# Attention scores as pairs of 64-row products, a weight check moved to late in the program, and a layer in halves

## The chip, the cores and the metric

One core of a Trainium2 chip runs the whole program. The metric is the time of one execution in device microseconds. Three timed runs of the kernel before gave 632.48, 632.51 and 632.81 us; their median, 632.51 us, is the time before. The engines that matter are PE (TensorE, the matrix engine; its loads of weights are listed as PEld), DVE (VectorE), ACT (ScalarE), POOL (GpSimd) and SP, whose queue issues all DMAs.

## What is computed

Attention over a short window with a few "sink" keys, then two feed-forward layers, on 2 x 768 tokens:

```python
batch, n_heads, seq, head_dim = (2, 8, 768, 64);  n_sink, window = (4, 128)
scores = scale * np.matmul(q, k.transpose(0, 1, 3, 2))
keep = is_sink | in_window                 # the last 128 keys and the first 4
a = softmax(np.where(keep, scores, -1e9))
x = np.matmul(a, v)                        # to (1536 tokens, 512)
h = x @ w_in;  x = (h * np.tanh(log1p(exp(h)))) @ w_out      # layer 0: 512 -> 2048 -> 512
h = x @ w2_in; out = (h * clip(h + 3, 0, 6) / 6) @ w2_out    # layer 1
```

q, k and v are float32. The four weight matrices come as float64.

## The kernel before

**Units and blocks.** A unit is 128 query tokens of one batch, with all 8 heads; there are 12, units 0 to 5 of the first batch and 6 to 11 of the second. Its window lies in its own 128 keys, those of the unit before, and the sinks. The first unit of a batch has one block of keys, the second has two, all later ones have two and 16 columns of sinks. Four units make a token block of 512 tokens, the width of one product in the two layers (`BLOCKS`, line 985).

**Early attention (`First`, lines 237 to 338).** Units 0 to 7 run first, in float32: `prep` transposes q and k on PE (line 251), `scores` multiplies (line 275, contraction over the 64 numbers of a head, so 64 of PE's 128 rows; odd heads sit in rows 64 to 127), takes the masked minimum on DVE (line 276) and the exponential on ACT (line 280); `turn` transposes the weights of the softmax (line 291), `values` multiplies by v (line 317), `normalise` and `outputs` divide and transpose into `xt` (lines 326, 332). Four heads make a group; each head's scores go to a PSUM bank of the pool `ps_h` (three banks), the output `o` to the one bank of `ps_s`.

**Layers (`up`, `down`, `moe_steps`).** float32 values are held as pairs of float16, so that a product becomes three (hi x hi, hi x lo, lo x hi). A step takes two of the 16 tiles of the hidden width: `up` makes 24 products into two `ps_h` banks (lines 646 to 648), ACT and DVE make the activation (lines 650 to 670), and `down` makes 24 products into the four accumulators (line 705), one step late (`LAG = 1`). `STAGES` (line 978) sets the order: layer 0 on block 0 and 1 in parts, as weights and attention come in, then block 2, then layer 1 on blocks 0, 1 and 2, each over all 16 tiles. Where a stage does not reach tile 16, `finish` copies its sums out (line 717) and a later stage adds them (line 721).

**Weights (`gen_decode`, lines 178 to 201).** Each of 32 tiles (two loads of 512 KB) is turned from float64 bits into pairs of float16 by five DVE and two ACT operations. The first DVE operation (line 185) and one on ACT (line 186) only check that the exponents are in range; their sums decide at the very end whether a general path has to run. Two raw buffers (`STB = 2`) hold what is loaded, and the 16 decoded buffers hold one layer, so that layer 1's tiles wait until layer 0's last block has used the same buffer.

**Late attention (`gen_front`, `gen_back`).** Units 8 to 11 run beside layer 0, in pieces that `hook` calls four times a step. Keys and queries are split into float16 pairs and transposed by DMA. For scores, a head's keys lie as (hi | lo) over the 128 rows and its queries as (lo | hi), so that one product over 128 rows makes both cross terms (line 465) and a second over 64 rows makes hi x hi (line 466):

```python
for t1, w_ in segs:                      # own keys (128 columns), previous keys and sinks (144)
    nc.tensor.matmul(sp[:, c:c + w_], qt[:, h, :], t1[:, h, 0:w_], start=True, stop=False)
    nc.tensor.matmul(sp[:, c:c + w_], qh[r0:r0 + 64, h // 2, :], t1[r0:r0 + 64, h, 0:w_], start=False, stop=True)
```

**What sets the order.** Each engine runs its instructions in the order in which the tile framework's scheduler put them, and each waits on semaphores of others. All DMAs stand in one queue, SP's, in the scheduler's order. A buffer of a pool is handed on when its last reader is done.

Of the kernel before, what the change touches and what calls it, by code (L numbers as in the profile page):

```python
# [17 lines left out]
SQ = 11      # powers of two that place float32 values in the range of float16 pairs  # L18
SK = 11
# [10 lines left out]
def attention_moe_moe2(  # L30
# [41 lines left out]
    blocks = BLOCKS  # L72
    order = sum(blocks, [])
    first = [u for u in range(NU) if u in sum(blocks[:2], [])]
# [12 lines left out]
    # previous block and sinks in it | own block | previous block | sinks  # L87
# [6 lines left out]
    # what the fast path relies on: lows[:, i] at least 1 in some partition, bads[:, i] 0 in all  # L94
# [28 lines left out]
    def emit_masks():  # L123
# [6 lines left out]
        # kept: 0 <= q - k < window in the block itself  # L130
# [14 lines left out]
        # which of four heads a row of the sink chunk belongs to: (row % 64) // 16  # L145
# [18 lines left out]
    def load_w():  # L164
        if nload[0] >= len(wseq):
            return
        layer, f = wseq[nload[0]]
        nload[0] += 1
# [7 lines left out]
        raw_t[layer, f] = t  # L176

    def gen_decode(idx):
# [3 lines left out]
        # nonzero where the exponent doesn't lie in float32's range below 2  # L182
        y = dec_p.tile([128, 1024], I16, tag="y", name="y")
        top = t.rearrange("p f t -> p (f t)").bitcast(I16).rearrange("p (f t) -> p f t", t=4)[:, :, 3]
        nc.vector.tensor_scalar(out=y, in0=top, scalar1=0x7800, scalar2=0x3800, op0=ALU.bitwise_and, op1=ALU.bitwise_xor)  # L185
        nc.scalar.activation(out=y, in_=y, func=AF.Copy, accum_out=wchk[:, idx:idx + 1])  # L186
# [50 lines left out]
    class First:  # L237
# [25 lines left out]
        def scores(self, g):  # L263
# [5 lines left out]
            for hh in range(4):  # L269
                h = 4 * g + hh  # L270
                rows = slice(64 * (h % 2), 64 * (h % 2) + 64)
                sp = ps_h.tile([128, n], F32, tag="h", name="s")
# [3 lines left out]
                nc.vector.tensor_tensor_reduce(  # L276
                    out=d[:, hh, 0:n], in0=sp, in1=self.mask, scale=SCALE, scalar=BIG,
                    op0=ALU.add, op1=ALU.min, accum_out=self.mins[:, h:h + 1],
                )
                nc.scalar.activation(  # L280
                    out=d[:, hh, 0:n], in_=d[:, hh, 0:n], func=AF.Exp, scale=-1.0,
                    bias=self.mins[:, h:h + 1], accum_out=self.sums[:, h:h + 1],
                )
# [20 lines left out]
        def values(self, g):  # L304
            if g == 0:
                self.o = ps_s.tile([128, H, D], F32, tag="so", name="o")
# [95 lines left out]
    def gen_keys(u):  # L402
        # heads in pairs: keys (hi lo | lo hi); values as pairs of float16
        b, i = divmod(u, NSB)
        kn, vn = (qkv_n.pop((u, nm)) for nm in "kv")
        k16 = late["at1"].tile([128, HP, 4, D], F16, tag="k16", name="k16")
        kp = kn.rearrange("p (a b) d -> p a b d", b=2)
        khi, klo = k16[:, :, 0::3, :], k16[:, :, 1:3, :]
        nc.scalar.activation(out=khi, in_=kp, func=AF.Copy, scale=2.0 ** SK)
        for h in range(2):  # L410
            nc.vector.scalar_tensor_tensor(out=klo[:, :, h], in0=kp[:, :, h], scalar=2.0 ** SK, in1=khi[:, :, h], op0=ALU.mult, op1=ALU.subtract)
        kt[u] = late["kv"].tile([128, H, 144], F16, tag="kt1", name="kt1")
        nc.sync.dma_start_transpose(out=kt[u][:, :, 0:128], in_=k16.rearrange("p a t d -> p (a t d)"))
# [11 lines left out]
    def gen_front(u):  # L425
# [9 lines left out]
        # queries (lo hi | hi lo)  # L435
        q16 = at1_p.tile([128, HP, 4, D], F16, tag="q16", name="q16")
# [586 lines left out]
```

## Time and profile before

| | |
|---|---|
| timed runs, median | 632.51 us (632.48 to 632.81) |
| profiled execution, span from first to last instruction | 636.4 us |
| PE busy | 617.9 us, 97% of the span |
| DVE busy | 373.3 us, 59% |
| ACT busy | 363.3 us, 57% |
| SP's DMA queue | 55.23 MB, 33.1% of 16 engines |
| late score products, lines 465 and 466 | 128 |
| weight check, lines 185 and 186 | 32 on each of DVE and ACT |

The profile shows one execution; its span is 3.9 us longer than the median of the timed runs, and the page gives no other time for it. A product's recorded duration includes the way through the array, which overlaps the next product: 512 columns are listed at about 380 ns and follow each other every 0.216 us. What a product costs is therefore read from starts, not from durations.

### The profile page before, as it was taken

To read this page: it belongs to the slowest core of one execution; us is meant where nothing else is said; L and a number is where in the kernel's file an instruction comes from. 1 tells how busy PE (TensorE), PEld (TensorE's weight loads), DVE (VectorE), ACT (ScalarE), POOL (GpSimd) and SP (SyncE) were. 2 spreads that over 40 slices of the span, in tenths; PEclk is the share of its full clock that TensorE was granted. 3 is DMA by queue.
4 is the path that set the end of the run, shared out by engine and by line. 5 is a ranking of instruction groups with operands and counts; after the bars stand their busy time and mean duration, and the time that the engine had idled before them with its cause. 6 is when DMAs were issued, how large, how long until landed. Compare 5 with 4: busy or idle time off the path is not lost.

```text
span 636.4 us, 8544 instructions
## 1 busy us (share of the span) xinstructions
PE 617.9 (97%) x3336; PEld 316.8 (50%) x3336; DVE 373.3 (59%) x694; ACT 363.3 (57%) x632; POOL 15.3 (2%) x28
## 2 busy tenths in 40 slices
PE   8999999989999999999999999999999999999995
PEld 4888865434454545444444444444444444444442
DVE  4687889977998753635789889852232222222221
ACT  5687798878878865665768865532141212422221
POOL 0200000600000000000000000000000000000000
PEclk8899999989999999999999999999999999999998
DMA  9747334988658603020134532300010000100001
GB/s 191 175 87 197 96 121 117 232 190 209 151 153 182 181 14 71 18 53 0 67 132 136 181 133 81 133 1 0 1 67 0 1 0 1 66 1 2 0 1 71
DMA packets 97256, 55.85 MB, mean 88 GB/s; under 512 B 75176, under 2 KB 91560, under 8 KB 97208
## 3 DMA queue, kind: packets, MB, share of 16 engines
q1 hardware_dynamic: 97208, 55.23, 33.1%
q8 instruction: 28, 0.46, 0.3%
q14 instruction: 20, 0.16, 0.1%
HBM read 43.65 MB, written 3.15 MB: 74 GB/s over the span
## 4 chain that ended last, share of the span: by engine, by line
PE 78%; DVE 8%; ACT 7%; DMA 4%; issue 2%; SPq 1%; ACTq 0%; DVEq 0%
PE acc L705 30%; PE h L646 11%; PE h L648 11%; PE h L647 11%; PE o L317 4%; PE s L275 4%; PE tp L291 2%; PE s L466 2%; DVE w L196 1%; DVE p L189 1%; DVE e L663 1%; ACT e L658 1%; ACT y L186 1%; PE tp L251 1%; PE s L465 1%
## 5 line engine op out<-in xcount | busy, mean ns | idle before, releaser
L646 PE MATMUL h<-xt,w 128*128 128x512 f16 x384 | 145.9, 380 | 2.0 <-DVE e L663 2.0
L647 PE MATMUL h<-xt,w 128*128 128x512 f16 x384 | 145.8, 380 | 0.0
L648 PE MATMUL h<-xt,w 128*128 128x512 f16 x384 | 145.6, 379 | 0.0
L705 PE MATMUL acc<-g,w 128*128 128x512 f16 x576 | 132.5, 381 | 1.0 <-DVE g L670 0.9
L705 PE MATMUL acc<-w,g 128*128 128x512 f16 x576 | 128.1, 379 | 0.0
L652 ACT ACTIVATE e<-h,bias 128x512 f32<-128x512 f32 x48 | 32.8, 685 | 136.1 <-PE h L648 136.1
L665 DVE SCALAR_TENSOR_TENSOR e<-e,h 128x512 f32<-128x512 f32 x48 | 33.0, 687 | 128.1 <-ACT e L652 128.1
L705 PEld LDWEIGHTS <-g 128*128 128x128 f16 x576 | 56.4, 98 | 67.9
L705 PEld LDWEIGHTS <-w 128*128 128x128 f16 x576 | 54.6, 98 | 65.5 <-issue 2.7
L670 DVE SCALAR_TENSOR_TENSOR g<-e,g 128x1024 f16<-128x1024 f32 x48 | 58.7, 1223 | 27.5 <-ACT g L669 27.4
L669 ACT ACTIVATE g<-e 128x1024 f16<-128x1024 f32 x48 | 50.6, 1054 | 32.6 <-DVE e L665 20.3
L647 PEld LDWEIGHTS <-w 128*128 128x128 f16 x384 | 37.6, 98 | 45.8 <-issue 2.9
L648 PEld LDWEIGHTS <-w 128*128 128x128 f16 x384 | 37.6, 98 | 44.8
L646 PEld LDWEIGHTS <-w 128*128 128x128 f16 x384 | 37.7, 98 | 43.6 <-issue 0.3
L650 ACT ACTIVATE e<-h 128x512 f32<-128x512 f32 x48 | 28.5, 593 | 32.7 <-PE h L648 32.5
L196 DVE SCALAR_TENSOR_TENSOR w<-p,w 128x1024 f16<-128x1024 f32 x32 | 39.2, 1224 | 11.7 <-ACT w L193 11.6
L186 ACT ACTIVATE y<-y 128x1024 int16<-128x1024 int16 x32 | 33.6, 1050 | 14.0 <-DVE y L185 14.0
L189 DVE SCALAR_TENSOR_TENSOR p<-raw,p 128x1024 int32<-128x1024 int32 x32 | 39.2, 1224 | 0.6
L190 DVE SCALAR_TENSOR_TENSOR p<-raw,p 128x1024 int32<-128x1024 int32 x32 | 39.1, 1222 | 0.2
L193 ACT ACTIVATE w<-p 128x1024 f16<-128x1024 f32 x32 | 33.6, 1049 | 5.7 <-DVE p L190 5.5
L663 DVE SCALAR_TENSOR_TENSOR e<-e,h 128x512 f32<-128x512 f32 x48 | 30.8, 681 | 9.8 <-ACT e L660 9.7
L280 ACT ACTIVATE d<-d,mins 128x272 f32<-128x272 f32 (+2 forms) x64 | 30.5, 480 | 3.7 <-DVE mins L276 3.6
(142 smaller groups left out, 619.3 us busy)
## 6 DMA issues: line engine op xcount, KB each, us to landing
raw<-in_moe_w_in_dram SPq DMA_DIRECT2D x32, 512.0 KB, 3.7
raw<-in_moe_w_out_dram SPq DMA_DIRECT2D x32, 512.0 KB, 4.7
out_dram<-ob SPq DMA_DIRECT2D x12, 256.0 KB, 2.1
first<-in_k_dram SPq DMA_DIRECT2D x8, 256.0 KB, 4.9
first<-in_q_dram SPq DMA_DIRECT2D x8, 256.0 KB, 5.0
first<-in_v_dram SPq DMA_DIRECT2D x8, 256.0 KB, 4.0
nk<-in_k_dram SPq DMA_DIRECT2D x5, 256.0 KB, 3.3
nv<-in_v_dram SPq DMA_DIRECT2D x5, 256.0 KB, 4.4
```

Source lines behind the costliest of these rows:

```text
L186: nc.scalar.activation(out=y, in_=y, func=AF.Copy, accum_out=wchk[:, idx:idx + 1])
L189: nc.vector.scalar_tensor_tensor(out=p, in0=lo_w, scalar=29, in1=p, op0=ALU.logical_shift_right, op1=ALU.bitwise_or)
L190: nc.vector.scalar_tensor_tensor(out=p, in0=hi_w, scalar=-0x40000000, in1=p, op0=ALU.bitwise_and, op1=ALU.bitwise_or)
L193: nc.scalar.activation(out=w[:, :, 0, :], in_=pf, func=AF.Copy, scale=2.0 ** SW)
L196: nc.vector.scalar_tensor_tensor(out=w[:, :, 1, :], in0=pf, scalar=2.0 ** SW, in1=w[:, :, 0, :], op0=ALU.mult, op1=ALU.subtract)
L646: nc.tensor.matmul(o, wh, x[:, 0, c, :], start=c == 0, stop=False)
L647: nc.tensor.matmul(o, wh, x[:, 1, c, :], start=False, stop=False)
L648: nc.tensor.matmul(o, wl, x[:, 0, c, :], start=False, stop=c == KD - 1)
L663: nc.vector.scalar_tensor_tensor(out=e[:, i], in0=e[:, i], scalar=2.5, in1=hps[i], op0=ALU.subtract, op1=ALU.mult)
L669: nc.scalar.activation(out=gh, in_=e, func=AF.Copy, scale=sc)
L670: nc.vector.scalar_tensor_tensor(out=gl, in0=e, scalar=sc, in1=gh, op0=ALU.mult, op1=ALU.subtract)
L705: nc.tensor.matmul(o, l_, r_, start=first and m == 0 and x == 0, stop=last and end and x == 2, skip_group_check=True)
```

## The change

- **Late scores**: keys and queries are laid out with the even head of a pair in rows 0 to 63 and the odd head in rows 64 to 127, hi and lo in separate columns. Each head now makes three 64-row products per block of keys (hi x hi, hi x lo, lo x hi), and the two heads' products alternate. Both heads' banks are filled before DVE takes the minima. `qh` and its transpose are gone.
- **Early scores**: two heads' products alternate in the same way.
- **PSUM**: `ps_s` is gone, `ps_h` has four banks, shared by scores, outputs `o` and the layers' `up`.
- **Units**: block 0 is units 6, 7, 0, 1; block 1 is 2 to 5; the early attention runs in that order.
- **Weight check**: layer 0's tiles are no longer checked while they are decoded. They are loaded a second time, from stage 8 on and after the last decode, and checked then. The ACT operation reads int32 words, half as many elements.
- **Layer 1 in halves**: blocks 0 and 1 take tiles 0 to 7, then tiles 8 to 15; block 2 all 16.

```diff
-    ps_h = main.enter_context(tc.tile_pool(name="ps_h", bufs=3, space=PSUM))
-    ps_s = main.enter_context(tc.tile_pool(name="ps_s", bufs=1, space=PSUM))
+    ps_h = main.enter_context(tc.tile_pool(name="ps_h", bufs=4, space=PSUM))
...
+    def exponents(idx, t):
+        y = dec_p.tile([128, 1024], I16, tag="y", name="y")
+        top = t.rearrange("p f t -> p (f t)").bitcast(I16).rearrange("p (f t) -> p f t", t=4)[:, :, 3]
+        nc.vector.tensor_scalar(out=y, in0=top, scalar1=0x7800, scalar2=0x3800, op0=ALU.bitwise_and, op1=ALU.bitwise_xor)
+        yy = y.bitcast(I32)
+        nc.scalar.activation(out=yy, in_=yy, func=AF.Copy, accum_out=wchk[:, idx:idx + 1])
+
+    def gen_check():
+        ahead = []
+        for f in range(KF):
+            ahead.append((f, fetch_w(0, f)))
+            if len(ahead) > STB - 1:
+                g, t = ahead.pop(0)
+                exponents(g, t.rearrange("p a f t -> p (a f) t"))
+            yield
...
     def gen_decode(idx):
...
+        if layer == 1:
+            exponents(idx, t)
...
-            for hh in range(4):
...
+            for h0 in (4 * g, 4 * g + 2):
+                sps = [ps_h.tile([128, n], F32, tag="h", name="s") for _ in range(2)]
                 for m, kv in enumerate(self.kvs):
                     w_ = n - 128 if m else 128
-                    nc.tensor.matmul(sp[:, m * 128:m * 128 + w_], self.qt[rows, h // 2, :], kv[0][rows, h // 2, 0:w_], start=True, stop=True)
+                    for r in range(2):
+                        rows = slice(64 * r, 64 * r + 64)
+                        nc.tensor.matmul(sps[r][:, m * 128:m * 128 + w_], self.qt[rows, h0 // 2, :], kv[0][rows, h0 // 2, 0:w_], start=True, stop=True)
...
-                sp = ps_s.tile([128, n], F32, tag="so", name="s")
...
+                sps = [ps_h.tile([128, n], F32, tag="h", name="s") for _ in range(2)]
                 c = 0
                 for t1, w_ in segs:
-                    nc.tensor.matmul(sp[:, c:c + w_], qt[:, h, :], t1[:, h, 0:w_], start=True, stop=False)
-                    nc.tensor.matmul(sp[:, c:c + w_], qh[r0:r0 + 64, h // 2, :], t1[r0:r0 + 64, h, 0:w_], start=False, stop=True)
+                    for tq, tk in ((0, 0), (0, 1), (1, 0)):
+                        for r in range(2):
+                            rows = slice(64 * r, 64 * r + 64)
+                            nc.tensor.matmul(
+                                sps[r][:, c:c + w_], qt[rows, tq * HP + h0 // 2, :], t1[rows, tk * HP + h0 // 2, 0:w_],
+                                start=tq + tk == 0, stop=tq == 1,
+                            )
...
-            ob = part_p.tile([128, DM], F32, tag="part", name="ob")
+            ob = a if span[0] > 0 else part_p.tile([128, DM], F32, tag="part", name="ob")
...
+            budget["chk"] = stage >= CHECK and not raw_t
...
-STAGES = [(0, 0, 0, 4), (0, 1, 0, 10), (0, 0, 4, 16), (0, 1, 10, 16), (0, 2, 0, 16), (1, 0, 0, 16), (1, 1, 0, 16), (1, 2, 0, 16)]
+STAGES = [(0, 0, 0, 4), (0, 1, 0, 10), (0, 0, 4, 16), (0, 1, 10, 16), (0, 2, 0, 16), (1, 0, 0, 8), (1, 1, 0, 8), (1, 0, 8, 16), (1, 1, 8, 16), (1, 2, 0, 16)]
+CHECK = 8
...
-BLOCKS = [[0, 1, 2, 3], [4, 5, 6, 7], [8, 9, 10, 11]]
+BLOCKS = [[6, 7, 0, 1], [2, 3, 4, 5], [8, 9, 10, 11]]
```

How this moves instructions is seen at three places. On PE, the scores of a late head before, between products of `up` (lines 646 and 648); `s` is the head's bank, `kt1` and `qt`, `qh` the transposed keys and queries:

```order
L648 MATMUL h_1632<-xt1_92,w_1230 128x512
L465 LDWEIGHTS qt_1519
L465 MATMUL s_1577<-kt1_1466,qt_1519 128x128
L466 LDWEIGHTS qh_1520
L466 MATMUL s_1577<-kt1_1466,qh_1520 128x128
L465 LDWEIGHTS qt_1519
L465 MATMUL s_1577<-kt1_1420,qt_1519 128x144
L466 LDWEIGHTS qh_1520
L466 MATMUL s_1577<-kt1_1420,qh_1520 128x144
```

Now, the first half of the first pair of late heads at the same kind of place:

```order
L668 MATMUL h_1500<-xt1_89,w_1111 128x512
L480 LDWEIGHTS qt_1489
L480 MATMUL s_1517<-kt1_1439,qt_1489 128x128
L480 LDWEIGHTS qt_1489
L480 MATMUL s_1518<-kt1_1439,qt_1489 128x128
L480 LDWEIGHTS qt_1489
L480 MATMUL s_1517<-kt1_1439,qt_1489 128x128
L480 LDWEIGHTS qt_1489
L480 MATMUL s_1518<-kt1_1439,qt_1489 128x128
```

Four products of one head have become twelve of two heads, which stand together with nothing between them at all 16 places and alternate between two banks.

On DVE, the middle of layer 1 before, where the last decode is over (line 665 is the activation of an `up` bank, line 670 the float16 remainder that `down` waits for):

```order
L670 SCALAR_TENSOR_TENSOR g_3938<-e,g_3938 128x1024
L196 SCALAR_TENSOR_TENSOR w<-p,w 128x2x512
L665 SCALAR_TENSOR_TENSOR e<-e,h 128x512 x2
L670 SCALAR_TENSOR_TENSOR g_4022<-e,g_4022 128x1024
L665 SCALAR_TENSOR_TENSOR e<-e,h 128x512 x2
L670 SCALAR_TENSOR_TENSOR g_4106<-e,g_4106 128x1024
```

The same place now (lines 685 and 690 are those two operations, line 184 the check of a tile that has just been loaded):

```order
L216 SCALAR_TENSOR_TENSOR w<-p,w 128x2x512
L690 SCALAR_TENSOR_TENSOR g_3925<-e,g_3925 128x1024
L184 TENSOR_SCALAR y<-raw 128x1024
L685 SCALAR_TENSOR_TENSOR e<-e,h 128x512
L184 TENSOR_SCALAR y<-raw 128x1024
L685 SCALAR_TENSOR_TENSOR e<-e,h 128x512
L184 TENSOR_SCALAR y<-raw 128x1024
L690 SCALAR_TENSOR_TENSOR g_3996<-e,g_3996 128x1024
L184 TENSOR_SCALAR y<-raw 128x1024 x2
```

Sixteen checks now stand between the activations of five steps, three or four to a step.

In SP's queue, the loads and transposes for the first late unit before, from the first load after the early attention:

```order
L387 DMA nk<-in_k_dram 128x8x64
L387 DMA nv<-in_v_dram 128x8x64
L498 DMA ksn<-in_k_dram 16x8x64
L511 DMA vsn<-in_v_dram 64x1x64 x4
L413 DMA_TRANSPOSE kt_1420<-k_1416 128x8x128
L171 DMA raw<-in_moe_w_in_dram 128x4x256
L506 DMA_TRANSPOSE ks_1355<-k16s 128x8x16
L175 DMA raw<-in_moe_w_out_dram 128x1024
L387 DMA nq<-in_q_dram 128x8x64
L387 DMA nk<-in_k_dram 128x8x64
```

And now:

```order
L411 DMA nk<-in_k_dram 128x8x64
L411 DMA nv<-in_v_dram 128x8x64
L520 DMA ksn<-in_k_dram 16x8x64
L411 DMA nq<-in_q_dram 128x8x64
L434 DMA_TRANSPOSE kt_1397<-k_1394 128x8x128
L411 DMA nk<-in_k_dram 128x8x64
L525 DMA_TRANSPOSE ks_1336<-k16s 128x8x16
L530 DMA vsn<-in_v_dram 64x1x64 x4
```

The loads of the query and of the second block of keys moved ahead of the sinks' values and of a tile of weights. On PE, 84 products of the layers now stand between the last early transpose (line 356) and the first late score; before it was 114.

## Rows read from the trace of the kernel before

**Rows 1.** The page, busy us by engine, share of the span, instructions.
```profile
PE 617.9 (97%) x3336; PEld 316.8 (50%) x3336; DVE 373.3 (59%) x694; ACT 363.3 (57%) x632; POOL 15.3 (2%) x28
```

**Rows 2.** Windows: stretch, length, busy us by engine (count), granted clock, DMA share, GB/s.
```profile
40.00:80.00 40.00, 39.85 (x352) 35.07 (x351) 32.33 (x106) 30.84 (x88) 0.00 (x0) 1.00 0.47 129
320.00:360.00 40.00, 38.68 (x179) 17.28 (x177) 36.03 (x40) 30.55 (x39) 0.00 (x0) 1.00 0.46 158
```

**Rows 3.** The chain that ended last, in layer 1: start us, us, what.
```profile
421.43 5.18 PE acc L705 x24
431.79 5.18 PE acc L705 x24
```

**Rows 4.** Timeline of PE, one late head: start us, us, engine, line, what.
```profile
135.75 0.22 PE L465 MATMUL s<-kt,qt 128*128 128x128 f16 x1
135.90 0.23 PE L466 MATMUL s<-kt,qh 64*128 64x128 f16 x1
136.06 0.24 PE L465 MATMUL s<-kt,qt 128*128 128x144 f16 x1
...
136.40 0.39 PE L646 MATMUL h<-xt,w 128*128 128x512 f16 x1
```

**Rows 5.** Timeline of PE, one group of four early heads.
```profile
35.48 1.20 PE L275 MATMUL s<-kt,qt 64*128 64x128 f32 x12
36.61 0.33 PE L332 MATMUL tp<-ident,xf 128*128 128x128 f32 x1
36.87 0.73 PE L275 MATMUL s<-kt,qt 64*128 64x128 f32 x4
37.54 0.55 PE L332 MATMUL tp<-ident,xf 128*128 128x128 f32 x3
```

**Rows 6.** Timeline of PE, two narrow windows, at 53.5 and at 54.3 us.
```profile
53.47 0.75 PE L275 MATMUL s<-kt,qt 64*128 64x128 f32 x8
...
54.04 0.63 PE L275 MATMUL s<-kt,qt 64*128 64x128 f32 x4
```

**Rows 7.** Waits of PE: who for whom, us in total, times, longest.
```profile
PE h L646 <- DVE e L663: 2.0, 2, 1.4
PE s L465 <- DMA qt<-q: 1.8, 1, 1.8
```

**Rows 8.** Timeline of SP's queue: start us, us of issuing, line, what.
```profile
103.94 0.37 SPq L387 DMA_DIRECT2D nk<-in_k_dram  x1
109.24 1.35 SPq L413 DMA_TRANSPOSE kt<-k  x1
121.67 1.27 SPq L413 DMA_TRANSPOSE kt<-k  x1
...
312.15 0.37 SPq L171 DMA_DIRECT2D raw<-in_moe_w_in_dram  x1
```

**Rows 9.** The chain, from 102 to 131 us and from 270 to 284 us.
```profile
114.59 5.13 DMA nk<-in_k_dram
126.03 4.19 DMA qt<-q
...
278.74 0.70 PE o L549 x24
```

**Rows 10.** Windows: behind the wait for the first late query.
```profile
131.00:134.00 3.00, 3.00 (x10) 1.12 (x10) 1.69 (x4) 2.45 (x5) 0.00 (x0) 0.53 1.14 243
```

**Rows 11.** Groups by line: count | busy us, mean ns of one | idle before.
```profile
L186 ACT ACTIVATE y<-y 128x1024 int16<-128x1024 int16 x32 | 33.6, 1050 | 14.0 <-DVE y L185 14.0
L185 DVE TENSOR_SCALAR y<-raw 128x1024 int16<-128x1024 int16 x32 | 22.0, 688 | 4.4 <-DMA raw<-in_moe_w_out_dram 4.3
L466 PEld LDWEIGHTS <-qh 64*128 64x128 f16 x64 | 5.9, 93 | 12.0 <-issue 9.2 <-DMA qh<-qh 0.4
```

**Rows 12.** Timeline of DVE in layer 1, after the last decode.
```profile
424.00 1.23 DVE L670 SCALAR_TENSOR_TENSOR g<-e,g 128x1024 f16<-128x1024 f32 x1 [1.12 <-ACT g L669]
```

**Rows 13.** The page, DMA issues: count, KB each, median us from issue to landing.
```profile
raw<-in_moe_w_out_dram SPq DMA_DIRECT2D x32, 512.0 KB, 4.7
```

More of the change, by code (lines that the diff above doesn't have):

```diff
@@ L67, in attention_moe_moe2 @@
     ps_acc = main.enter_context(tc.tile_pool(name="ps_acc", bufs=4, space=PSUM))
-    ps_h = main.enter_context(tc.tile_pool(name="ps_h", bufs=3, space=PSUM))
-    ps_s = main.enter_context(tc.tile_pool(name="ps_s", bufs=1, space=PSUM))
+    ps_h = main.enter_context(tc.tile_pool(name="ps_h", bufs=4, space=PSUM))
     blocks = BLOCKS
     order = sum(blocks, [])
-    first = [u for u in range(NU) if u in sum(blocks[:2], [])]
+    first = blocks[0] + blocks[1]
     last = sum(blocks[2:], [])
@@ L162, in attention_moe_moe2, with fetch_w @@
     nload = [0]
[L164 to L168, printed above, removed]
+    def fetch_w(layer, f):
         wi, wo = wsrc[layer]
@@ L175, in load_w @@
         nc.sync.dma_start(out=t[:, 1].rearrange("p f t -> p (f t)"), in_=wo[f * 128:(f + 1) * 128, :])
-        raw_t[layer, f] = t
+        return t
+    def load_w():
+        if nload[0] >= len(wseq):
+            return
+        layer, f = wseq[nload[0]]
+        nload[0] += 1
+        raw_t[layer, f] = fetch_w(layer, f)
+    def exponents(idx, t):
[12 more added lines that the diff above has]
+            yield
+        for g, t in ahead:
+            exponents(g, t.rearrange("p a f t -> p (a f) t"))
+            yield
     def gen_decode(idx):
@@ L305, in values @@
             if g == 0:
-                self.o = ps_s.tile([128, H, D], F32, tag="so", name="o")
+                self.o = ps_h.tile([128, H, D], F32, tag="h", name="o")
             fresh = g == 0
@@ L405, in gen_keys @@
         kn, vn = (qkv_n.pop((u, nm)) for nm in "kv")
[L406 to L413, printed above, removed]
+        k16 = late["at1"].tile([128, 2, H, D], F16, tag="k16", name="k16")
+        nc.scalar.activation(out=k16[:, 0], in_=kn, func=AF.Copy, scale=2.0 ** SK)
+        nc.vector.scalar_tensor_tensor(out=k16[:, 1], in0=kn, scalar=2.0 ** SK, in1=k16[:, 0], op0=ALU.mult, op1=ALU.subtract)
+        kt[u] = late["kv"].tile([128, 2 * HP, 144], F16, tag="kt1", name="kt1")
+        nc.sync.dma_start_transpose(out=kt[u][:, :, 0:128], in_=k16.rearrange("p t h d -> p (t h d)"))
         if i + 1 < NSB:
@@ L496, in gen_sinks @@
         at1_p = late["at1"]
-        ksn = at1_p.tile([16, H, D], F32, tag="q16", name="ksn")
+        ksn = at1_p.tile([128, 512], F32, tag="xf", name="ksn")[0:16].rearrange("p (h d) -> p h d", h=H)
         nc.sync.dma_start(out=ksn, in_=k[b, :, 0:16, :].rearrange("h p d -> p h d"))
-        k16 = at1_p.tile([16, HP, 4, D], F16, tag="qh16", name="k16s")
-        kp = ksn.rearrange("p (a b) d -> p a b d", b=2)
-        khi, klo = k16[:, :, 0::3, :], k16[:, :, 1:3, :]
-        nc.scalar.activation(out=khi, in_=kp, func=AF.Copy, scale=2.0 ** SK)
-        for h in range(2):
-            nc.vector.scalar_tensor_tensor(out=klo[:, :, h], in0=kp[:, :, h], scalar=2.0 ** SK, in1=khi[:, :, h], op0=ALU.mult, op1=ALU.subtract)
-        ks[b] = at1_p.tile([128, H, 16], F16, name=f"ks_{b}")
-        nc.sync.dma_start_transpose(out=ks[b], in_=k16.rearrange("p a t d -> p (a t d)"))
+        k16 = at1_p.tile([128, 2, DM], F16, tag="x16", name="k16s")[0:16].rearrange("p t (h d) -> p t h d", h=H)
+        nc.scalar.activation(out=k16[:, 0], in_=ksn, func=AF.Copy, scale=2.0 ** SK)
+        nc.vector.scalar_tensor_tensor(out=k16[:, 1], in0=ksn, scalar=2.0 ** SK, in1=k16[:, 0], op0=ALU.mult, op1=ALU.subtract)
+        ks[b] = at1_p.tile([128, 2 * HP, 16], F16, name=f"ks_{b}")
+        nc.sync.dma_start_transpose(out=ks[b], in_=k16.rearrange("p t h d -> p (t h d)"))
         yield
@@ L532, in gen_back @@
         at_p, at1_p = late["at"], late["at1"]
-        o = ps_s.tile([128, H, D], F32, tag="so", name="o")
+        o = ps_h.tile([128, H, D], F32, tag="h", name="o")
         for g in range(2):
@@ L622, in attention_moe_moe2 @@
     dec_side = Side(gen_weights())
+    chk_side = Side(gen_check())
     gt = {}
@@ L772, in hook @@
                 dec_side.piece()
+        if budget["chk"]:
+            chk_side.piece()
     def moe_steps():
@@ L814, in attention_moe_moe2 @@
     nc.vector.memset(ones, 1.0)
-    cnt = ps_s.tile([1, NLOW + 4], F32, tag="so", name="cnt")
+    cnt = ps_h.tile([1, NLOW + 4], F32, tag="h", name="cnt")
     nc.tensor.matmul(cnt[:, 0:NLOW], ones, lows, start=True, stop=True)
```

76 lines of the change are left out of this document (34 added, 42 removed).

## The prediction

> **What bounds the kernel now.** I read the page's busy times first. PE works 617.9 us of a span of 636.4, DVE and ACT less than 60% of it [rows 1]. So only what leaves PE's queue, or lets PE wait less, can shorten the program. Next I read windows. From 40 to 80 us, where the early attention runs, PE is listed busy for 39.85 of 40 us with DVE at 32.33 and ACT at 30.84; from 320 to 360, where layer 1's weights are decoded, PE has 38.68 and DVE 36.03, so DVE has almost nothing to spare there [rows 2]. The chain of waits says the same of layer 1: 24 `down` products take 5.18 us, 0.216 each, and begin 10.36 us apart, which is 48 x 0.216 [rows 3]. A step is nothing but its 48 products there; this stretch can only be spoilt.
>
> Busy is not the same as well used, though, and the timeline of PE shows it. A late head's four products begin at 135.75, and the next `up` product begins at 136.40: 0.65 us for (128 + 144) x 2 columns [rows 4]. At the rate of the long products (0.216 / 512 per column) these columns are worth 2 x 0.054 + 2 x 0.061 = 0.23 us. The other 0.42 has four places to come from: each product changes between 128 and 64 rows. I read 0.105 us per change. An early group of four heads shows another thing: its first twelve records take 1.13 us, its last four 0.67 [rows 5]. And elsewhere eight records of two heads take 0.75 us, four of one head 0.63 [rows 6]: products of two heads on different halves of the array run beside each other, a single head's run alone. A float32 product is two records.
>
> Then the waits of PE: 2.0 us for DVE's `e` before an `up` bank is free, and 1.8 us for the first late query [rows 7], behind which the clock is granted at 0.53, the lower level of 1.2 GHz, from 131 to 134 us [rows 10].
>
> The sum below is against the profiled execution, 636.4 us of span (the profile gives no other time for it), which is 3.9 above the timed median of 632.51. The terms are differences, so I take them off the median.
>
> **Late scores: -11.9 us.** 32 heads x 0.65 = 20.8 us go. In their place stand 16 groups of twelve 64-row products, six pairs. If the two of a pair run beside each other, as the early ones do [rows 6], a group costs 3 x 0.054 + 3 x 0.061 = 0.345, and two changes of row count, at its start and its end, 2 x 0.105: 0.555 us, x 16 = 8.9. Bounds: with no change cost at all 16 x 0.345 = 5.5 (-15.3); if every product costs what one costs now, 0.65 / 4 = 0.16, 192 of them make 31 (+10). In between, pairs one after the other make 0.69 + 0.21 = 0.90, x 16 = 14.4 (-6.4). I choose the first, nearest to the row that shows two halves at once.
>
> That needs each product's weights to be loaded in time. A weight load of such a product is listed at 93 ns [rows 11], longer than its 54. But 24 products of attention's output, each with its own loads, take 0.70 us, 29 ns each [rows 9], so loads go beside products there. The Trainium skill, "TensorE: Matmul & The Clock Gate", "Part 3: Packing small matmuls", says that a load of weights overlaps products in flight only when its row group differs; by that rule the alternation of halves would hide at most every load behind the other half's product, and rule and the 29 ns do not agree, since those loads use the same rows. What the rule would make of the time is the second rival.
>
> **Early scores: -4.5 us.** A full group costs 1.13 + 0.67 = 1.80 now; wholly paired it is two of 54.04 - 53.47 = 0.57, 1.14, so 0.65 less. There are twelve such groups (six units with two blocks of keys). The first group of a unit finds four free banks and gains 0.65; in the second the output `o` holds one, so that its second pair waits for a minimum of DVE: I give it 0.1. 6 x 0.75 = 4.5. Ends: all twelve at 0.65, -7.8; pairs that wait for banks, +2. ACT and DVE have 8 to 9 us of 40 to spare there [rows 2], so they follow.
>
> **Banks: -2.0 us.** The 2.0 us of waiting for `e` [rows 7] lie in layer 0's last block and in the decode. A fourth bank for `up` takes them. Ends: -2.9 (with the rest of the 1.3 that PE loses from 320 to 360 [rows 2]) and +2.
>
> **First late query: -0.5 us.** Now: keys are loaded at 103.94, transposed by DMA from 109.24 [rows 8], the second keys' load lands at 114.59 + 5.13 = 119.72, its transpose is issued at 121.67, and the query's takes from 126.03 to 130.22 [rows 8, 9]. PE came 24.3 us after that first load and waited 1.8. Changed, counting from the first load: the second keys' load is issued behind the first transpose, 5.3 + 1.35 = 6.65 (it moves ahead of the sinks' values and a weight tile), lands 5.13 later, 1.95 to its transpose, 1.27 of issuing, 4.19 for the query's: 19.2. PE comes 30 products earlier (84 in place of 114), 24.3 - 6.5 = 17.8, and waits 1.4, with the low clock as before. Ends: no wait and no low clock, -3.5 (1.8, and 47% of some 3.6 us); the weight tile's or the sinks' loads in the way after all, +6.5.
>
> **Weight check: +1.5 us.** Layer 0's sixteen checks leave the time when PE sets the pace: nothing gained, 16 x 0.69 on DVE and 16 x 1.05 on ACT [rows 11] were beside PE's work. Now they come in layer 1, with a second load of 1 MB each, in about five steps, 51.8 us. Two buffers: a tile's first load takes 0.37 to issue [rows 8] and 4.7 to land [rows 13], 5.1, then 0.69 for the check, 5.8, and with two in flight 2.9. DMA alone: 158 GB/s at a share of 0.46 [rows 2] makes 343 in full, 1 MB in 3.05 us, x 16 = 49. So the tiles just keep up. DVE waits in its queue for a tile, and behind it stand the activations that `down` waits for; before, DVE ended at 425.23 [rows 12] what `down` needs at 431.79 [rows 3], 6.5 us to spare. A step with four tiles needs 12.2 us, 1.8 over; I take 1.5 once. Ends: 0, and the slow rival's 35.
>
> **New stalls: +3 us.** `up`, `o` and scores now share four banks, where scores had their own. Two pairs that meet an `up` bank in use cost 1.0 each, as the two waits of [rows 7] did: +2 (0, to half of 16 pairs, +8). With 30 `up` products fewer before the last early transposes these are covered less: +1 (0 to 2).
>
> **Nothing** for the layer in halves: its copies and adds lie beside PE, in the 6.5 us [rows 3, 12]; without that cover each of eight would stop PE for about 1 us. It also gives the decode of tiles 8 to 15 more time. Nothing for the order of the units (the same products) nor for the conversions saved.
>
> Sum: -11.9 - 4.5 - 2.0 - 0.5 + 1.5 + 3 = -14.4, or 618.1 us. I say **618**; this case's own range is 612 to 624.
>
> **Rivals.**
> 1. *Pairs run one after another* in the late scores: -6.4 in place of -11.9, 623.6. For it: the early rows are float32, none of before are float16 on halves. Against: nothing in [rows 6] depends on the type. 10%.
> 2. *Loads of weights do not overlap*: a product costs its load and itself, 0.093 + 0.055, and if one of each pair hides, a pair costs 0.148: 96 x 0.148 + 16 x 0.21 = 17.6, a gain of 3.2, 626.8. That is the rule of the Trainium skill named above at its hardest. Against it stand the 29 ns [rows 9]. 6%.
> 3. *Early scores give nothing*, since banks or ACT bind: +4.5, 622.6. For it, the one bank of `o`; against, DVE's and ACT's spare time [rows 2]. 12%.
> 4. *More than I think*: no change cost (-3.4), all early groups (-3.3), no first wait (-3): 608.4. 5%.
> 5. *Slower: the check holds DVE.* If the two buffers' loads do not overlap, a tile takes 5.8 us, sixteen 93; five steps and the slack cover 51.8 + 6.5, and 34.6 falls on PE, less the 1.5 counted: 651. It decides from 4.6 us a tile, (58.3 + 15.9) / 16, where the gains are eaten. For it: the loads are in one queue, and a buffer is free only after DVE's check. Against: at 320 to 360 us, two buffers moved 158 GB/s with a decode between [rows 2]. 12%, of which 4% near no change.
>
> **Chances and range.** The forecast has 55%. What a measurement of this kernel can tell from no change is 0.2%, 1.3 us. Faster: 55 + 10 + 6 + 12 + 5 = 88%; within it 4%; slower 8%. The range of 608 to 630 takes in rivals 1 to 4 and leaves out the slower cases and a little at the low end.
>
> **What would show it.** Twelve score products in about 0.55 us between two `up` products; 0.9 means rival 1, over 1 rival 2. An early group in 1.1 to 1.7 us. Among PE's waits no `up` <- DVE `e` above 1 us, and the first late query's wait near 1.4 with a low clock behind it. Checks on DVE every 3 us from about 400 us on, ended by DMA; where they come every 5 to 6 us, and PE waits for DVE's `g` by tens of us, rival 5 is right. The forecast is wrong if PE's steps in layer 1 come more than 10.5 us apart, or if PE's waits in the first 130 us grow by more than 3.

## The result: 8.9 us off, where 14.4 were forecast

Changed, the kernel takes 623.66 us (median of four runs, 623.01 to 626.35); before, 632.57 on the same chip. The ratio is 0.984, 95% interval 0.981 to 0.988. The time lies in the forecast range and, just, in the likeliest case's own range. It keeps to the latter by 0.34 us, less than the four runs differ by, so that is luck. The sum was 5.5 us too large, and the table below shows which terms made it so.

The execution of before that is shown ahead of the prediction was a long one: its clock stood at the lower level from 12 to 22 us and from 131 to 135. A second profile of the unchanged kernel (run e1: 632.47 us, span 630.7) has no such stretch, and the profile after has none either (623.05 us, span 621.3). So these two are compared. The page after, in the columns of [rows 1]:

```profile
PE 600.8 (97%) x3400; PEld 307.6 (50%) x3400; DVE 376.0 (61%) x688; ACT 354.6 (57%) x640; POOL 14.2 (2%) x28
```

To see where time went I cut each trace by PE's own work. At a mark I take the start time and subtract 0.216 us for each 512-column product of the layers started before it; what is left is everything that is not such a product at the full clock. The differences from mark to mark, in us (the last column is the span itself):

```
                        early      to first  first to   to 672nd  to 1152nd  to 1344th  span
                        attention  late      last late  product   product    product
                                   score     score
shown ahead             93.16      2.21      28.44      0.17      6.51       0.48       636.4
e1 (before again)       89.01      2.35      26.56      0.17      6.47       0.47       630.7
after                   88.77      2.06      17.98      1.08      5.07       0.85       621.3
e2 by threes            89.12      2.22      17.95      1.08      5.16       0.87       622.3
e3 early serial         90.01      2.67      20.22      1.08      5.02       1.06       626.0
e4 old units            91.27      1.85      19.73      1.08      5.21       0.87       625.6
e5 same half            88.72      2.03      22.71      1.08      4.88       0.85       626.4
e6 check at decode      90.41      2.44      21.01      1.08      5.26       0.85       626.8
e7 layer 1 whole        88.64      1.82      17.98      1.08      5.45       0.86       621.7
e8 scores only          92.52      2.73      18.63      1.08      7.48       0.85       628.8
e9 sinks between        88.98      1.67      22.87      1.08      5.17       0.87       626.9
e10 tail cover          88.77      2.57      20.95      1.08      5.40       0.86       625.2
e11 sinks and tail      90.59      1.90      19.48      1.08      5.06       0.87       625.1
e12 no late check       89.10      2.03      17.95      1.08      5.14       0.88       621.9
```

From e1 to after the program gains 8.6 us in the late attention and next to nothing in the early attention, where 4.5 were forecast. The two columns behind the last late score have to be read together: 24 products of the last unit's output, 0.92 us, stand just behind the mark between them in e1 (263.89 us) and just ahead of it after (254.12). Together they are 6.64 in e1 and 6.15 after, and the next column takes 0.38 of that back. From the 1344th product on the two differ by 0.2.

**The late scores** after, in the timeline of PE, answer to [rows 4]:

```profile
122.19 0.38 PE L668 MATMUL h<-xt,w 128*128 128x512 f16 x1
122.50 0.53 PE L480 MATMUL s<-kt,qt 64*128 64x128 f16 x12
122.96 0.60 PE L725 MATMUL acc<-g,w 128*128 128x512 f16 x2
```

Twelve products take 0.46 us from start to the next product's, and the product ahead of them lasts 0.31 in place of 0.216: 0.46 + 0.095 = 0.555 us, to the digit what was forecast.

**An early group of four heads**, first in e1, then after, each with the product of the sinks' values (`o` from `vsb`, 64 rows) that follows it:

```profile
43.14 1.20 PE L275 MATMUL s<-kt,qt 64*128 64x128 f32 x12
44.27 0.66 PE L332 MATMUL tp<-ident,xf 128*128 128x128 f32 x4
44.85 0.48 PE L310 MATMUL o<-vsb,ats 64*128 64x256 f32 x1
44.86 0.48 PE L275 MATMUL s<-kt,qt 64*128 64x128 f32 x2
45.17 0.38 PE L310 MATMUL o<-vsb,ats 64*128 64x256 f32 x1
45.19 0.41 PE L275 MATMUL s<-kt,qt 64*128 64x144 f32 x2
45.52 0.32 PE L317 MATMUL o<-first,at 128*128 128x64 f32 x1
```

```profile
47.56 1.21 PE L296 MATMUL s<-kt,qt 64*128 64x128 f32 x16
48.70 0.66 PE L356 MATMUL tp<-ident,xf 128*128 128x128 f32 x4
49.28 0.70 PE L334 MATMUL o<-vsb,ats 64*128 64x256 f32 x2
49.91 0.32 PE L341 MATMUL o<-first,at 128*128 128x64 f32 x1
```

The scores did shrink, from 1.13 + 0.67 to 1.14 us. But before, the last head's four records and the sinks' two ran beside each other in those 0.67 us; after, the sinks' two run alone for 0.63. From the first row of a fence to its last it is 2.38 us before and 2.35 after. Three of the four such groups of e1 are like this; in the fourth, the group of [rows 5], the sinks' product comes later and alone.

Ahead of the transposes of the last unit but one (line 332 at 89.95 us in e1, line 356 at 90.38 after) PE has started 48 `up` products, in e1 36: twelve more, worth 2.6 us, in 0.43 us more, so it is 2.2 us ahead. Then the last unit comes. With the new order it is one with sinks, and it has no scores beside it:

```profile
90.91 0.70 PE L334 MATMUL o<-vsb,ats 64*128 64x256 f32 x2
...
94.90 0.70 PE L334 MATMUL o<-vsb,ats 64*128 64x256 f32 x2 [0.38 <-DVE ats L326]
```

Two of these products, 0.63 each to the next start, with the wait of 0.38 ahead of one, are 1.6 us that e1's last unit doesn't have. At the end of the early attention 0.24 of the 2.2 is left.

**The waits of PE** after, against [rows 7]:

```profile
PE acc L725 <- DVE g L690: 2.2, 2, 1.4
PE s L480 <- DMA qt<-q: 1.8, 1, 1.8
PE s L480 <- DVE mins L487: 1.6, 2, 1.4
PE o L557 <- DMA atg<-ag: 1.6, 1, 1.6
PE h L666 <- DVE e L683: 1.3, 1, 1.3
```

And in e1, for the same three:

```profile
PE h L646 <- DVE e L663: 2.0, 2, 1.4
PE o L538 <- DMA atg<-ag: 1.2, 1, 1.2
PE acc L705 <- DVE g L670: 0.9, 2, 0.5
```

The two waits for `e` of e1 lie at 306.9 and 349.4 us, in the last block of layer 0 and in the decode, and are gone. The one of 1.3 that after has lies among the late scores, at 140.5. But where e1 waits for `e`, after waits for `g`, DVE's next result: 1.4 us at 322.6 and 0.7 at 364.9 (and 0.55 for ACT's `g` at 299.9).

Waits for minima (`mins`) are new: in e1 they came to 0.2 us at these scores. How one comes about stands in DVE's timeline, and under it PE's:

```profile
183.06 0.69 DVE L208 TENSOR_SCALAR p<-raw 128x1024 int32<-128x1024 int32 x1
183.79 1.23 DVE L209 SCALAR_TENSOR_TENSOR p<-raw,p 128x1024 int32<-128x1024 int32 x1
184.93 0.43 DVE L487 CUSTOM_DVE_ANT_0 d<-s,m_all 128x272 f32<-128x272 f32 x1
```

```profile
185.42 0.21 PE L480 MATMUL s<-kt,qt 64*128 64x128 f16 x1 [1.45 <-DVE mins L487]
```

The minimum takes 0.43 us, but it stands behind two decode operations of a weight tile in DVE's queue. The next pair needs the bank that it reads.

**The weight check** in layer 1, DVE's timeline (two neighbours and the last, of sixteen; the first is at 399.60), and the windows:

```profile
404.20 0.69 DVE L184 TENSOR_SCALAR y<-raw 128x1024 int16<-128x1024 int16 x1 [1.63 <-DMA raw<-in_moe_w_out_dram]
407.99 0.69 DVE L184 TENSOR_SCALAR y<-raw 128x1024 int16<-128x1024 int16 x1 [1.04 <-DMA raw<-in_moe_w_out_dram]
...
449.46 0.69 DVE L184 TENSOR_SCALAR y<-raw 128x1024 int16<-128x1024 int16 x1 [2.46 <-DMA raw<-in_moe_w_out_dram]
```

```profile
400.00:440.00 40.00, 40.00 (x188) 18.12 (x185) 17.64 (x24) 18.50 (x40) 0.00 (x0) 1.00 0.93 322
```

Sixteen checks come 3.3 us apart ((449.46 - 399.60) / 15), DMA is busy for 0.93 and moves 322 GB/s, and PE is busy for all of the 40 us. PE's list of waits is empty from 380 us to 600.

### The profile page after: what moved, and what is told of

The parts are those of the page before. It is cut to its first block, busy times and chain, and to the rows that moved or that the text cites. A ratio compares the mean times of both kernels' runs of the same rounds, so it can differ in the third digit from the quotient of the medians.

```text
span 621.3 us, 8731 instructions
## 1 busy us (share of the span) xinstructions
PE 600.8 (97%) x3400; PEld 307.6 (50%) x3400; DVE 376.0 (61%) x688; ACT 354.6 (57%) x640; POOL 14.2 (2%) x28
## 4 chain that ended last, share of the span: by engine, by line
PE 68%; DVE 14%; ACT 9%; DMA 4%; issue 3%; SPq 1%; ACTq 0%; DVEq 0%
PE acc L725 27%; PE h L666 9%; PE h L668 9%; PE h L667 9%; PE o L341 4%; PE s L296 3%; DVE g L690 2%; DVE e L683 2%; PE tp L315 2%; DVE p L209 2%; DVE p L210 2%; ACT w L213 1%; ACT e L678 1%; ACT e L679 1%; DVE w L216 1%
## 5 line engine op out<-in xcount | busy, mean ns | idle before, releaser
L725 PE MATMUL acc<-g,w 128*128 128x512 f16 x576 | 129.5, 379 | 2.7 <-DVE g L690 2.2
L186 ACT ACTIVATE y<-y 128x512 int32<-128x512 int32 x32 | 20.0, 625 | 37.0 <-DVE y L184 36.9
```

The costliest lines, as they stand in the source:

```text
L725: nc.tensor.matmul(o, l_, r_, start=first and m == 0 and x == 0, stop=last and end and x == 2, skip_group_check=True)
```

## The experiments

Each is the kernel after with one edit, unless said; times are medians of 4 to 12 runs, ratios against the kernel before on the same chip. After itself stands at 0.984 (0.981 to 0.988). One execution of each kernel was traced, and executions of one kernel differ by 1.6 to 4.7 us (after 623.01 to 626.35, e7 623.47 to 628.20; e1 by 6.1), so a row of the table is one execution and not the kernel's median.

**e1: the kernel before again.** 

> The kernel before, unchanged, for the span and granted clock of each of its executions. Theory A: its profiled execution (span 636.4 us) was a slower one than the timed ones, because PE's clock stood at its lower level from 11.7 to 21.9 us; the executions timed here then have spans near 630.8 (the timed 632.5 less the 1.75 us that lies around the span of the kernel after), a mean clock near 0.995, and a profile without that stretch. Rival B: the low stretch is there in every execution, and the 5 us lie around the span. Then the spans are near 636 with the clock at 0.987.

632.47 us in the profiled execution, span 630.7, clock 0.998; the median of the twelve is 633.27 (631.91 to 638.04). Two of them had a span near 636 and a clock of 0.986, the other ten spans of 630.1 to 632.8. Theory A holds: the rows ahead come from an execution like those two. The low stretches go with 93.16 - 89.01 = 4.2 us in the early part and 1.9 in the late one, where a minimum is also waited for 0.4 us longer.

**e2: late products by threes.** 

> The kernel after, with the late scores' twelve 64-row products in another order: all six of the even head, then all six of the odd one; banks and minima as before. Theory A (two halves run beside each other): a group of twelve goes from 0.46 to about 0.46 + 0.35 = 0.81 us, 16 groups cost 5.5 us more, 629 us. Rival B (what was saved is only the change between 128 and 64 rows, the halves don't matter): within 1 us of 623.7.

```diff
-                    for tq, tk in ((0, 0), (0, 1), (1, 0)):
-                        for r in range(2):
+                    for r in range(2):
+                        for tq, tk in ((0, 0), (0, 1), (1, 0)):
```

625.32 us, 0.988 (0.984 to 0.991). The edit does less than was expected of it: the loop over blocks of keys stays outside, so the order is three products of the even head, three of the odd, and again. A group still takes 0.47 us:

```profile
146.10 0.54 PE L480 MATMUL s<-kt,qt 64*128 64x128 f16 x12
146.57 0.60 PE L725 MATMUL acc<-g,w 128*128 128x512 f16 x2
```

In the trace the first products of the two heads start within about 0.01 us of each other, though three places apart in the program. So this run doesn't test the halves; it shows that PE finds the pairs by itself.

**e5: both heads on the same half.** 

> The kernel after, but the two heads whose late products alternate are two even ones, then two odd ones, so that both use the same half of the array's rows; number, size, banks and minima as after. Theory A (the pairs of after run beside each other on the two halves, and that is worth something): a group of twelve goes from 0.46 to 12 x 0.058 + 0.1 = 0.8 us, and 16 groups add 5.4 us: 629. Rival B (halves don't matter, only the changes between 128 and 64 rows that are gone): within 1 us of 623.7. Rival C (the rule that a load of weights is hidden only behind a product on other rows): each product pays its load, 0.093 + 0.055, a group 1.8 us, and 16 groups add 21 us: 645.

```diff
-            for h0 in (4 * g, 4 * g + 2):
+            for h0 in (4 * g, 4 * g + 1):
-                            rows = slice(64 * r, 64 * r + 64)
+                            rows = slice(64 * (h0 % 2), 64 * (h0 % 2) + 64)
```

(and the second head is `h0 + 2`). 627.40 us, 0.991 (0.988 to 0.993).

```profile
124.45 0.88 PE L480 MATMUL s<-kt,qt 64*128 64x128 f16 x12
125.26 0.61 PE L725 MATMUL acc<-g,w 128*128 128x512 f16 x2
```

0.81 us for the same twelve, as theory A had it. The two halves are worth 0.35 us a group, 5.6 in all, and the time is 3.7 longer. The late stretch of the trace adds up: 5.6 for the groups, 1.7 for a low stretch of the clock from 120.4 to 123.8 us that after's trace doesn't have, and 2.6 less in stalls, together the 4.7 of the table. Theory C, the load of weights in the open, falls: products on the same rows follow each other every 0.055 to 0.067 us.

**e3: early scores head by head.** 

> The kernel after, with the early scores head by head in place of pairs; banks as after. Theory A (pairing the early scores is worth the 0.65 us a group seen in the trace, where a group of four heads went from 1.79 to 1.14): about 4.5 us slower, 628. Rival B (the early part is bound by ACT, DVE or the loads, so that PE's gain is lost in waits): within 1 us of 623.7.

```diff
-                for m, kv in enumerate(self.kvs):
-                    for r in range(2):
+                for r in range(2):
+                    for m, kv in enumerate(self.kvs):
```

626.36 us, 0.989 (0.985 to 0.992). Its groups take 1.24 us in place of 1.14, no more: again PE finds most pairs itself, once four banks are free (e1, head by head with three banks, has 1.80). The early part has 1.2 us more, the late one 2.2, though PE's instructions there are those of after. Neither 4.5 nor 0, and not all of it is the pairs': the interval overlaps that of after, the clock was low from 98.6 to 105.4 us, and DVE's order in the late stretch is another (see e9).

**e4: the old order of units.** 

> The kernel after with the old order of units (block 0 is units 0 to 3, block 1 units 4 to 7). Theory A (the order of units is worth nothing): within 1.2 us of 623.7. Rival B (the units with fewest products first spare the clock's low stretch at the start or give back waits): 2 to 5 us slower, with a low clock in the first 25 us or more waiting before the first late query.

```diff
-BLOCKS = [[6, 7, 0, 1], [2, 3, 4, 5], [8, 9, 10, 11]]
+BLOCKS = [[0, 1, 2, 3], [4, 5, 6, 7], [8, 9, 10, 11]]
```

628.00 us, 0.992 (0.989 to 0.995): 4.3 slower than after. Rival B is right in size, by other signs than it named. PE waits 2.6 us at the end of the early attention for ACT's copies, where after has 0.2:

```profile
PE o L341 <- ACT at L317: 2.6, 2, 1.6
```

In e1, with this order too, twelve `up` products stand there between the last transposes and most of the values; with the four shared banks they don't. Behind these stops, from 98.2 to 105.0 us, the clock was at its lower level. The mean clock is 0.988 to 0.990 in all six executions, where after has 0.992 to 0.998. Of the 4.3 us of span that the traces differ by, 2.5 lie in the early attention and 1.75 in the late stretch, whose order on DVE is that of e3.

**e6: the check at the decode, e7: layer 1 whole, e8: both and the old units.** 

> The kernel after, with all 32 weight checks at the decode, as before (the int32 form of the ACT operation kept), and no second load of layer 0's weights. Theory A (the check is hidden beside PE's work in either place): within 1.2 us of 623.7. Rival B (its absence lets the decode and the late attention of layer 0 run with fewer waits of PE between 100 and 300 us): 2 to 4 us slower, 626 to 628, by waits of PE in that stretch.

> The kernel after, with layer 1's blocks 0 and 1 each over all 16 tiles in one stage, as before; the late check begins with block 1. Theory A (the halves move copies and adds that are hidden, and nothing else): within 1.2 us of 623.7. Rival B (the halves give the decode of layer 1 time, and without them PE waits for it between 300 and 400 us, by 2 us or more): 626 or more.

> The kernel after with three of its parts undone at once: old order of units, check at the decode, layer 1 not in halves; new are the scores and the four shared banks. Theory A (of those three only the order of units is worth anything, 4.3 us as measured by itself): 628, within 1.2 of the run with the old order of units. Rival B (each of the three gives a part): 630 or more, little better than the kernel before.

```diff
-        if layer == 1:
-            exponents(idx, t)
+        exponents(idx, t)
-            budget["chk"] = stage >= CHECK and not raw_t
+            budget["chk"] = False
```

e6 takes 628.25 us, 0.992 (0.989 to 0.994), with 1.6 more in the early part and 3.0 more in the late; rival B fits in size, but not only for its reason: 1.7 of the 3.0 are a low stretch of the clock from 162.2 to 165.7 us, the clock was low from 97.4 to 104.2 too, and DVE's order is another. e7 takes 624.32, 0.988 (0.984 to 0.991): theory A. e8 takes 629.84, 0.994 (0.992 to 0.995): rival B by size. Scores and banks alone thus bring 3 us of the 9. The three parts together bring 6, where the three taken away singly cost 4.3 + 4.6 + 0.7. From 672 to 1152 e8 has 7.48, after 5.07, e6 5.26 and e7 5.45, as if halves and late check each spared the same waits. But in e8 the clock was low behind a stop of PE of 1.4 us:

```profile
329.00:332.00 3.00, 3.00 (x9) 1.08 (x8) 2.91 (x3) 2.94 (x5) 0.00 (x0) 0.50 0.00 0
```

Its products there start every 0.43 us in place of 0.216, which makes 1.7 us; the 5.8 that are left are 0.3 above e7. That the two parts spare the same waits is not shown.

**e9, e10, e11: sinks beside the scores, `up` behind the last transposes, both.** 

> The kernel after, with the early product of the sinks' values (line 334, 64 rows) issued between the two pairs of scores of a unit's first group, next to four score products; after, the transposes of an output stand between them. Theory A (the early scores gained nothing in time since the kernel before ran this product beside the last scores, and after runs it alone, 0.63 us): a group of scores and sinks takes 0.3 to 0.5 less, three such groups 1 to 1.5 us, 622.3. Rival B (the bank that the output then holds earlier makes the second pair wait for a minimum of DVE): nothing gained, 623.7 to 625.

> The kernel after, with the second 24 up products of the layers issued behind the last transposes of the early attention instead of ahead of them. Theory A (PE's stops of 0.38 and 0.23 us there, with the 0.79 behind them, are what lets the clock fall to its lower level from 96 to 105 us in some executions; covered, they and it go): a span of 620.5, the runs within 1 us of each other, median 622.5. Rival B (the stops are hidden by the wait for the first late query anyway, and the clock is granted by something else): within 1 us of 623.7, with the same spread.

> Both of the two edits before: the sinks' product beside the scores, and the up products behind the last transposes. Theory A (they touch different places of PE's order): the two gains add, 621 to 622. Rival B (the first late query is waited for anyway, so that what is gained before it is lost there): no better than the better of the two.

```diff
+                if between is not None and h0 % 4 == 0:
+                    between()
...
-                f.scores(0)
+                f.scores(0, lambda: e.sinks(0))
```

```diff
-            if f is None:
-                next(moe)
...
-            if n == len(us) - 2:
+            if n >= len(us) - 2:
                 next(moe)
```

626.78, 627.41 and 626.92 us; ratios 0.989 (0.987 to 0.991), 0.991 (0.989 to 0.993) and 0.990 (0.988 to 0.991). The medians are 3.1 to 3.8 us above that of after, and every theory A here fell; so did rival B in e9 and e10, while e11 is no better than e9, as its rival had it. In e9 the sinks' product does run beside scores:

```profile
47.54 0.74 PE L296 MATMUL s<-kt,qt 64*128 64x128 f32 x8
48.21 0.33 PE L362 MATMUL tp<-ident,xf 128*128 128x128 f32 x1
48.57 0.45 PE L336 MATMUL o<-vsb,ats 64*128 64x256 f32 x1
48.83 0.37 PE L296 MATMUL s<-kt,qt 64*128 64x128 f32 x1
48.86 0.38 PE L336 MATMUL o<-vsb,ats 64*128 64x256 f32 x1
49.05 0.66 PE L296 MATMUL s<-kt,qt 64*128 64x128 f32 x7
49.63 0.55 PE L362 MATMUL tp<-ident,xf 128*128 128x128 f32 x3
50.02 0.33 PE L347 MATMUL o<-first,at 128*128 128x64 f32 x2
```

But from scores to values it is 2.48 us, against 2.35 after and 2.38 in e1: split in two, the scores cost more changes of rows, and nothing is left of the gain. In e10 the stops of 0.38 and 0.23 us are gone, and the clock is at 0.52 from 99 to 102 us all the same. What e9 and e10 lose, they lose in the late stretch, 22.87 and 20.95 us against 17.98, where PE's instructions are those of after but for some fourteen `down` products at its start:

```profile
PE s L489 <- DVE mins L496: 3.6, 2, 1.9
PE acc L734 <- DVE g L699: 1.3, 2, 0.9
PE h L675 <- DVE e L692: 1.0, 1, 1.0
```

(e9, 119 to 256 us.) After has 1.6, nothing and 1.3 there. Two things differ in this stretch that no edit names. One is the clock, low for 3.4 us in e9 (189.9 to 193.3) and in e10 (187.9 to 191.3), each time behind a stop of 1.9 us:

```profile
190.00:193.00 3.00, 3.00 (x9) 1.04 (x8) 2.54 (x8) 2.44 (x6) 0.00 (x0) 0.50 0.62 179
```

That is 1.7 us in e9 and 1.6 in e10. The other is DVE's order. Ahead of the minimum that is waited for longest, e9 has a weight check (line 184) between two decode operations, which follow each other directly in after:

```profile
182.49 1.22 DVE L210 SCALAR_TENSOR_TENSOR p<-raw,p 128x1024 int32<-128x1024 int32 x1
183.63 0.69 DVE L184 TENSOR_SCALAR y<-raw 128x1024 int16<-128x1024 int16 x1
184.83 1.23 DVE L216 SCALAR_TENSOR_TENSOR w<-p,w 128x1024 f16<-128x1024 f32 x1 [0.52 <-ACT w L213]
```

Compared operation by operation, the traces of after, e5, e7 and e12 have one order of DVE's 167 recorded operations from the first late score to the last. In e3 and e4 some fifty of them stand elsewhere, in the same order in both; in e9, e10 and e11 some 35, again in one order; in e6 some 80. The edits are in the early attention (in e6 in the decode too), but the scheduler, which sets the order, moved DVE's decode against its minima in the stretch behind them.

**e12: no late check.** Layer 0's check and its second loads are left out. 

> The kernel after without the check of layer 0's sixteen weight tiles and without their second load; this part of the check is left out, its sums are set to zero. Theory A (the late check is hidden wholly beside PE's products of layer 1): within 0.5 us of the kernel after in span and time. Rival B (DVE held for the tiles costs PE what was forecast, 1.5 us): 622.2, with PE's waits for g before 450 us shorter by as much.

623.89 us, 0.986 (0.984 to 0.988), span 621.9 against 621.3: theory A by the medians, and the waits for `g` are those of after. The late check costs nothing that can be measured.

## Why the prediction was partly right

- **Late scores, forecast -11.9.** Right in mechanism and size. Added up by PE's starts, they take 20.9 us in e1 and 12.6 after. 16 x 0.555 = 8.9 of the 12.6 are the products and their two changes of rows, and 3.7 are stalls. e5 shows what the halves give of it, 0.35 us a group. The rival of weight loads in the open (626.8) is refuted: in e5 neighbours use the same rows, each load is listed at 94 ns, and still a product comes every 0.055 to 0.067 us. The Trainium skill, "TensorE: Matmul & The Clock Gate", "Part 3: Packing small matmuls", says that a load of weights overlaps products in flight only when its row group differs; the measurement is otherwise, and it decides here.
- **Early scores, forecast -4.5.** This step failed; 0.24 came. "A full group costs 1.13 + 0.67 = 1.80 now; wholly paired [...] 1.14, so 0.65 less" holds for the group that was read, [rows 5], but not for "twelve such groups": in three of four with sinks the 0.67 us were shared with the sinks' product, and the gain is 0.03. In the second groups the second pair does wait for a minimum, as forecast (1.94 us with the sinks' product, in e1 and after alike). Of the 2.2 us by which after is ahead at 90 us, the last unit, with its sinks alone on PE, leaves 0.24. Rival 3 had this time for the term, but its reason, the bank of `o` or ACT, is only part of it.
- **Banks, -2.0, and new stalls, +3.** The first of these steps failed. The 2.0 us of waiting for `e` are gone, as forecast, but "A fourth bank for `up` takes them" is wrong about the path: PE waits for DVE's and ACT's `g` in their place, 2.7 us (0.55, 1.43, 0.73) where e1 has 1.0, and 0.4 longer for the DMA of `atg`. From the last late score to the 1344th product it is 7.0 us after and 7.1 in e1, so 0.1 came of the 2.0. The stalls at the late scores cost 3.7 - 0.3 = 3.4 us (e1 has 0.3 of such stalls). Together +3.3 against +1.0: right in sign, 2.3 us too good. The forecast priced two such waits at 1.0; two came, at 1.4 (`up` for `e`, against the sign that no such wait would be above 1 us) and 1.9 (a minimum), and a third of 0.4. That these are the price of the shared banks is read from who waits for whom; no run has the pairs and a bank of the scores' own.
- **First late query, -0.5.** -0.3; the wait is 1.8 us where 1.4 was forecast. Its low clock did not have to come: e1 waits 1.9 us and keeps the clock.
- **Weight check, +1.5.** 0 (e12). Tiles came every 3.3 us, the forecast's 3.05 and a little; DVE's slack took all of it. Rival 5, the check that holds DVE, needed 4.6.
- **Nothing for the order of the units.** Wrong taken by itself: with new scores and banks the old order costs 4.3 us (e4). Right for the sum, where new order and shared banks come together: the new order takes back the 2.6 us of stops at the end of the early attention, to which the prediction gave 1 us. The rest of the 4.3 goes with the low clock and DVE's other order behind them.

By the spans of e1 and after the gain is 9.4 where 14.4 were forecast, and the terms make up the difference: 4.3 (early scores), 2.3 (banks and stalls) and 0.2 (first query) too good, 1.5 (check) too bad, and 0.2 gained behind the 1344th product.

What stays open is the late stretch. It takes 17.95 to 17.98 us in after, e2, e7 and e12, 18.6 in e8, and 19.5 to 23 in e3, e4, e6, e9, e10 and e11. The waits are for DVE, which is busy 17 to 19 of each 20 us from 120 to 200 us in after. The slowest six have another order on DVE, and e6, e9 and e10 a low clock of 1.6 to 1.7 us besides. But e2, where some 16 operations stand elsewhere, loses nothing, and e9, e10 and e11, with one order, differ by about 2 us after the clock is taken off; no run changes DVE's order alone. So neither the 3.0 us of e6 nor the 2.2 of e3 can be put down to its edit.

## What to carry over

Before you count what a shorter group of products gains, look who else runs in its time: a half-empty array may already be filled by a neighbour in the queue, and the sum from the group's start to the next full-width product is what counts. When pools are merged, a bank comes free when another engine's queue gets to its reader: the price is the longest pieces ahead of that reader (here 0.69 + 1.23 us of decode before 0.43 of a minimum), not the reader. A wait that goes away may only have moved: where the engine waited for is full, add up the stretch and not the one wait. And look at two executions before a sum is made against one: two executions of the kernel before differ by 5.7 us here, most of it low stretches of the clock. Before a difference is put down to an edit, look in both traces for such stretches, and at the order of the engines that the edit doesn't name.

## Not expected of the hardware

- PE runs products on different halves beside each other also when they are three places apart in the program (e2, 0.47 us a group), and in float32 when head follows head (e3, 1.24 against 1.14). Within a group the written order matters little; with four banks in place of three, and DVE's minima behind both heads' scores, the early group went from 1.80 to 1.24 (e1, e3).
- Twelve products of 64 rows with a load each take 0.46 us on two halves and 0.81 on one. A change between 128 and 64 rows costs about 0.095 us, read where the product ahead of a group lasts 0.31 us in place of 0.216.
- A low stretch of the clock can come or not behind the same stop of PE (the wait for the first late query, 1.77 us in e5 and 1.80 after, both at 119 us). In e5, e6, e8, e9 and e10 it begins 0.2 to 1.6 us behind a stop of 1.4 to 1.9 us and lasts 3.4 us; after has stops of 1.80 and 1.45 us and keeps its clock.
- Among products of the layers such a stretch costs 1.6 to 1.7 us. Near 100 us it can cost next to nothing: in e12 the clock was granted at 0.50 from 99 to 102 us, and the wait for the first late query was 0.5 us in place of 1.8.

```profile
99.00:102.00 3.00, 3.00 (x10) 1.53 (x10) 2.35 (x4) 1.54 (x2) 0.00 (x0) 0.50 0.74 164
```
